# Seven-product first layer in a seventh chunk of a sorted-attention and expert-mixture kernel, with weight sums partly by adding transfers

## The chip, the core and the metric

The kernel runs on one core of a Trainium2 chip. The core has TensorE (PE, matrix multiply; its weight loads are listed apart as PEld), VectorE (DVE), ScalarE (ACT), GpSimd (POOL) and SyncE (SP); SP and POOL also issue transfers, which run on the core's 16 DMA engines. The time is the device time of the launch in microseconds, and the smaller the better.

## The reference

Block-sorted attention gives `x` (4 batches of 768 tokens, 512 wide), and four experts with weights per token give the output. What matters here is the second part:

```python
N, D, E, F = (3072, 512, 4, 1024)
p = domain_probs / (domain_probs.sum(-1, keepdims=True) + 1e-09)
out = np.zeros((N, D), dtype=np.float32)
for e in range(E):
    h = np.maximum(x @ w1[e], 0.0)
    out += p[:, e:e + 1] * (h @ w2[e])
```

The first layer is `x @ w1[e]`, the second layer `h @ w2[e]`.

## The kernel before

**Tiles and stages.** The 3072 tokens are worked off in 12 chunks of 256 tokens, three for each batch; chunk number `g` is batch `g // 3`, part `g % 3`. A chunk runs the first layer of all four experts into `Hb` (fp16, four blocks for each expert: two halves of the hidden width by two halves of the tokens), and then the second layer over all experts at once. The attention of later batches is woven into the chunks of batches 0 and 1, so that batches 2 and 3 have no attention left beside their chunks.

**Second layer.** A 2 x 2 block product in seven products instead of eight. Its sums of `w2` blocks are made once in place and in `T_e`; its sums of `Hb` blocks are made for each chunk by VectorE (`h_sums`, L734) into `Sb`, which has four areas `sm(0)` to `sm(3)`: `h_sums(e, 3)` writes `sm(2)`, `h_sums(e, 4)` writes `sm(3)`. The seven products are called b11, b21, n4, t1, t2, t3, b22 after the weight block that they use.

**First layer, two forms.** The plain form (`chunk_first`, L759) takes 32 matmuls of 256 columns for each expert, in two groups of 16; VectorE evicts a group by one instruction that applies ReLU and the token weight `pb` (L774). The seven-product form (`seven`, L1022) treats the layer as 2 x 2 blocks too: seven products p1 to p7, each 8 matmuls of 128 columns (L1032), linked by copies on ACT (L1052, L1059, L1067) and sums on VectorE (L1068, L1076). Two of the four result blocks are finished by VectorE (`finish`, L1038), two by ReLU on ACT and a multiplication on POOL (`finish2`, L1044 and L1045).

The seven-product form needs four sums of `w1` blocks for each expert (`input_sums`, L961): s1 = a21 + a22, s3 = a11 - a21, s2 = s1 - a11, s4 = a12 - s2. The first three lie in blocks of 1024 columns of `arena`, where the attention has its inputs, its mixing matrices and its output copy; s4 overwrites a21 in `w1`. It also needs four sums of token blocks for each chunk (`token_sums`, L975).

**Order.** Every engine runs its instructions in program order; the order was written by hand. In the chunks of batches 0 and 1, `chunk` (L783) calls `slot()` at fixed places: after each group of the first layer (slots 0 to 7) and after each product of the second layer (slots 8 to 14). `PLANS` names the attention steps for each (part, slot), and `PLAN_A` (L1175) the weight sums. With G0 = 6 (L972), chunks 3, 4 and 5 of batch 1 run in `chunk` with the plain form for all experts, and chunks 6 to 11 in `last_chunk` (L1088) with the seven-product form for all experts. `prepare_last` and `last_banks` close the attention's PSUM pool, then the chunks' pool, and open new ones for the seven-product form; each opening has one dummy matmul (L1000). `last_begin` (L1083) puts the first products of the next chunk's expert 0 ahead of the end of the present chunk.

**Buffers.** The temporaries of `seven` (u2, u3, t22, t12) lie in buffers that the attention no longer uses: a slot of the tag "xT", two of "vs" and one of "xsl". The normalised attention of the last two head pairs of batch 3 (`st_a`, L430) lies in `arena` blocks 4 and 5. The token weights `pb` have one buffer, loaded anew for each chunk by SP (L213).

Of the kernel before, what the change touches and what calls it, by code (L numbers as in the profile page):

```python
# [17 lines left out]
def kernel(  # L18
# [411 lines left out]
    def st_a(b, pr):  # L430
        if b == B - 1 and pr >= H // 2 - 2:
            xsl = arena[:, ds((pr + 2) * NB * 2 * D, NB * 2 * D)].rearrange("p (i h d) -> p i h d", i=NB, h=2)[0:BLK]
        else:
            xsl = att.tile([P, NB, 2, D], F16, name=f"xsl_{b}_{pr}", tag="xsl")[0:BLK]
        xsls[(b, pr)] = xsl
        vs = vss[(b, pr // 2)]
        for hh in range(2):
            ET = ETs[2 * (pr % 2) + hh]
            ps = psa([P, 2, 512], F32, f"ps_a_{b}_{pr}_{hh}")
            for i in range(NB):  # L440
                nc.tensor.matmul(  # L441
                    ps[:, i // HB, ds((i % HB) * VW, D + 1)],
                    ET[:, ds(i * BLK, P)],
                    vs[:, i, 2 * (pr % 2) + hh, 0:D + 1],
                    start=True, stop=True,
                )
            normalize(ps, xsl, hh)
# [286 lines left out]
    def h_sums(e, which):  # L734
        blk = lambda kh, tok: Hb[:, e, ds(kh * KH, KH), ds(tok * P, P)]
        sm = [Sb[:, n, e].rearrange("p (f x) -> p f x", f=KH) for n in range(4)]
        tt = nc.vector.tensor_tensor
        if which == 1:
            tt(sm[0], blk(0, 1), blk(1, 1), ALU.add)  # L739
        elif which == 2:  # L740
            tt(sm[1], sm[0], blk(0, 0), ALU.subtract)
        elif which == 3:
            tt(sm[2], blk(0, 0), blk(0, 1), ALU.subtract)
        else:
            tt(sm[3], blk(1, 0), sm[1], ALU.subtract)
# [37 lines left out]
    def chunk(b, c, slot, done=()):  # L783
# [13 lines left out]
        def product(n, lhs, rhs, pool=psm):  # L797
            ps = pool([P, DH], F32, f"ps_{n}_{b}_{c}")
            for e in es:
                if pool is last_bank and e == 2:  # L800
                    last["e0"][6]()
                for f in range(KH):
                    nc.tensor.matmul(  # L803
                        ps[:], lhs(e, f), Ts[e][rhs][:, f, :],
                        start=(e == es[0] and f == 0), stop=(e == E - 1 and f == KH - 1),
                    )
            return ps[:]
# [13 lines left out]
        if b or c:  # L821
            two = [psm([P, 2, 512], F32, f"ps_p{n}_{b}_{c}") for n in range(2)]
            bankA, bankB, bankC, bankQ = [two[n // 2][:, n % 2, 0:DH] for n in range(4)]
            if last:
                bankQ = last["Q"][1][:, 0:DH]
        if b:
            times(bankA, blk(0, 0), "b11", es)
            slot()
            times(bankB, blk(1, 0), "b21", es)
            slot()  # L830
            nc.scalar.copy(p1[:], bankA)
            tt(oa1, bankB, p1[:], ALU.add)
            times(bankQ, sm(0), "t1", es)
            nc.scalar.copy(p5[:], bankQ)
            slot()
            for e in es:
                h_sums(e, 3)
            times(bankA, sm(1), "t2", es, False)
            nc.scalar.copy(u2[:], bankA)
            slot()  # L840
            for e in es:
                h_sums(e, 4)
            times(bankC, blk(1, 1), "n4", es)
            nc.scalar.copy(ob1, bankC)
            slot()
            times(bankA, sm(2), "t3", es, False)
            tt(ob2, bankA, p5[:], ALU.add)
            tt(ob1, bankA, ob1, ALU.add)
            store(1, ob)
            slot()  # L850
            times(bankQ, sm(3), "b22", es, False, True, last["e0"][6] if last else None, 2 if last else None)
            tt(oa2, bankQ, u2[:], ALU.add)
            slot()
            store(0, oa)
            return
# [91 lines left out]
    def a_block(n):  # L947
        return arena[:, ds(n * AW, AW)].rearrange("p (k f) -> p k f", k=2)


    A_ORDER = (6, 7, 8, 0, 1, 2, 3, 4, 5, 9, 10, 11)
    As = []
    for e in range(E):
# [4 lines left out]
            "s1": a_block(A_ORDER[3 * e]), "s3": a_block(A_ORDER[3 * e + 1]), "s2": a_block(A_ORDER[3 * e + 2]),  # L958
        })

    def input_sums(e, n, half=None):  # L961
        a = As[e]
        dst, x, y, op = (
            ("s1", "a21", "a22", ALU.add), ("s3", "a11", "a21", ALU.subtract),
            ("s2", "s1", "a11", ALU.subtract), ("s4", "a12", "s2", ALU.subtract),
        )[n]
        part = slice(None) if half is None else slice(half, half + 1)
        nc.vector.tensor_tensor(a[dst][:, part], a[x][:, part], a[y][:, part], op)
# [3 lines left out]
    G0 = 2 * (R // 2)  # L972
    GN = B * (R // 2)

    def token_sums(g):  # L975
# [7 lines left out]
            "t1": t3[:, 0], "t2": t3[:, 1], "t3": t3[:, 2],  # L983
            "t4": wide[g % 2][:, 0:2 * P].rearrange("p (k x) -> p k x", k=2),
        }
        for dst, x, y in (("t1", "b12", "b11"), ("t2", "b22", "t1"), ("t3", "b22", "b12"), ("t4", "b21", "t2")):
            nc.vector.tensor_tensor(t[dst], t[x], t[y], ALU.subtract)
# [14 lines left out]
    def prepare_last():  # L1002

        last_banks(0)
        last["n"] = 1
        t = moe.tile([P, NKC, NB, BLK], F16, name="tmp7", tag="xT").rearrange("p k i x -> p (k i x)").bitcast(F32)
        room = [t[:, ds(n * 512, 512)] for n in range(3)]
        for m in range(2):
            t = att.tile([P, NB, 4, VW], F16, name=f"tmp7_{m}", tag="vs").rearrange("p i h w -> p (i h w)")
            t = t[:, 0:2048].bitcast(F32)  # L1010
            room += [t[:, 0:512], t[:, 512:1024]]
        t = att.tile([P, NB, 2, D], F16, name="tmp7_2", tag="xsl").rearrange("p i h d -> p (i h d)").bitcast(F32)
        room.append(t)
        for n, nm in enumerate(("u2", "u3", "t22", "t12")):
            last[nm] = room[2 * n:2 * n + 2]

    def last_bank(shape, dtype, name):
        n = last["n"]
        last["n"] += 1
        return last["Q"][2 - n % 2][:, 0:shape[1]]  # L1020

    def seven(g, e):  # L1022

        a, t, pb = As[e], Bs[g], pbs[divmod(g, R // 2)]
        X, Z, u2, u3, t22, t12 = [last[nm][e % 2] for nm in ("X", "Z", "u2", "u3", "t22", "t12")]
        X, Z, Q = X[:], Z[:], last["Q"][e][:]
# [30 lines left out]
        def p6():  # L1057
            product(X, "s2", "t2")
            nc.scalar.copy(u2, X)  # L1059
# [28 lines left out]
    def last_chunk(g):  # L1088
        b, c = divmod(g, R // 2)
        final = g == GN - 1  # L1090
        last["e0"][2]()
        if g == G0:
            last_banks(1)
        prs = [last["e0"]] + [seven(g, e) for e in range(1, E)]
        for e in range(1, E):
# [3 lines left out]
            if e > 1:  # L1099
                prs[e - 2][12]()  # L1100
# [6 lines left out]
            for n in late_sums.pop((g, e), ()):  # L1107
                input_sums(*n)
# [25 lines left out]
        nc.scalar.copy(p1[:], bankA)  # L1134
        now[3]()
# [7 lines left out]
        if final:  # L1143
            nc.sync.dma_start(o[:, 2 * c, 0:DH], oa1)
        h_sums(E - 1, 1)
# [3 lines left out]
        nc.scalar.copy(ob1, bankC)  # L1149
        for e in range(E):  # L1150
            h_sums(e, 4)
        product(bankQ, sm(0), "t1")
        nc.scalar.copy(p5[:], bankQ)
        product(bankA, sm(1), "t2", False)
        nc.scalar.copy(u2[:], bankA)
        for e in range(E):
            h_sums(e, 3)
        product(bankQ, sm(3), "b22", False, range(2))
        if not final:
            token_sums(g + 1)  # L1160
        product(bankA, sm(2), "t3", False)
        if not final:
            last_begin(g + 1)
# [3 lines left out]
        product(bankQ, sm(3), "b22", False, range(2, E), None if final else last["e0"][6], 3)  # L1167
# [8 lines left out]
        (1, 11, 0, 0), (1, 13, 0, 1), (2, 1, 0, 2), (2, 3, 1, 0), (2, 5, 1, 1), (2, 7, 1, 2),  # L1176
        (2, 8, 2, 0), (2, 9, 2, 1), (2, 10, 2, 2), (2, 10, 0, 3), (2, 11, 1, 3), (2, 11, 3, 0), (2, 12, 2, 3),
        (2, 13, 3, 1), (2, 14, 3, 2),
    ]
    late_sums = {(G0, 1): [(3, 3, 0)], (G0, 2): [(3, 3, 1)]}  # L1180
# [112 lines left out]
    for b in range(2):  # L1293
        for c in range(R // 2):
            done = (1, 2) if (b, c) == (0, 0) else ()
            at = [2 * len(done)]

            def slot(b=b, c=c, at=at):
                here = (c, at[0])
                for cc, n, f, *args in PLANS[b]:  # L1300
                    if (cc, n) == here:
                        f(*args)
                if b:
                    for cc, n, e, m in PLAN_A:
                        if (cc, n) == here:
                            input_sums(e, m)
                    if here == (R // 2 - 1, 7):
                        prepare_last()
                    if here == (R // 2 - 1, 12):
                        token_sums(G0)  # L1310
                    if here == (R // 2 - 1, 13):
                        last_begin(G0)
                at[0] += 1

            chunk(b, c, slot, done)
    for g in range(G0, GN):
# [29 lines left out]
```

The softmax here doesn't subtract the row's maximum and nothing guards it: scores larger than these inputs give would overflow.

## Time and profile before

| | us |
|---|---|
| median of 3 runs | 366.0 (365.18 to 366.91) |
| profiled execution, whole time | 364.59 |
| profiled execution, span from first to last instruction | 362.5 |

The granted clock of TensorE is 1.0 in the profiled execution. Some instants of its timeline, in us from the span's start:

| what | from | to |
|---|---|---|
| first matmul of chunk 5 (plain first layer) | 183.66 | |
| second layer of chunk 5, product b11 | 197.90 | |
| chunk 6, first product of expert 0, inside the end of chunk 5 | 208.38 | |
| second layer of chunk 6, product b11 | 222.13 | |
| same, chunk 7 | 246.86 | |
| last transfer issued by POOL (attention input) | 138.4 | 139.1 |
| POOL's first multiplication in `finish2` | 215.82 | |

How to read the profile: a row of a timeline has the start, the length, the engine, the line of the program, the operation, what it writes and reads with the shape, and how many instructions were merged; in brackets the idle time before it and what ended that. A row of windows has the window, its length, and then the busy time and the number of instructions of PE, PEld, DVE, ACT and POOL, the granted clock, the busy share of the DMA engines and GB/s. A row of transfers has the issuing queue, the number, the size of each and the median time from issue to landing. A row of waits has who waited for whom, the total, the number of times and the longest.

### The profile page before, as it was taken

What the parts mean: (1) busy time and instruction counts of PE and PEld (TensorE: products, weight loads), DVE (VectorE), ACT (ScalarE), POOL (GpSimd) and SP (SyncE); (2) the same over time, 40 slices, a digit from 0 to 9 for tenths busy, and PEclk for the clock granted to TensorE, in tenths of its full rate; (3) what the DMA queues carried; (4) which work ended last, traced back from release to release, by engine and by line L of the source; (5) the groups of instructions that cost most, each with busy time, mean ns of one, the idle gap of its engine ahead of it and who ended that gap; (6) DMA issues with size and microseconds to landing.
All of it is one profiled execution on the core that took longest, in us unless ns stands there. A gap on an engine that the chain in (4) does not pass through costs nothing.

```text
span 362.5 us, 10556 instructions
## 1 busy us (share of the span) xinstructions
PE 354.1 (98%) x4517; PEld 314.6 (87%) x4517; DVE 280.0 (77%) x559; ACT 157.7 (44%) x282; POOL 117.5 (32%) x134
## 2 busy tenths in 40 slices
PE   8799999999999999999999999999999999999996
PEld 8685857888888888988888899999999998999995
DVE  5753898779798676866799979868779679587794
ACT  2664430452424355367400157165283381561740
POOL 8882011655022420000000018137055082180470
PEclk9999999999999999999999999999999999999999
DMA  8999999999999999934450310310301101102101
GB/s 109 206 208 230 208 210 200 194 186 158 175 197 162 210 91 172 161 85 73 85 126 2 58 60 4 58 60 4 88 31 49 71 2 60 61 2 65 55 16 44
DMA packets 69753, 38.34 MB, mean 106 GB/s; under 512 B 40390, under 2 KB 64716, under 8 KB 69708
## 3 DMA queue, kind: packets, MB, share of 16 engines
q0 software_dynamic: 34640, 17.83, 38.5%
q1 hardware_dynamic: 35068, 19.85, 27.0%
q8 instruction: 35, 0.57, 0.6%
q14 instruction: 10, 0.08, 0.1%
HBM read 42.00 MB, written 6.34 MB: 133 GB/s over the span
## 4 chain that ended last, share of the span: by engine, by line
PE 86%; DVE 6%; DMA 5%; issue 1%; ACT 1%; POOL 1%; DVEq 0%; ACTq 0%
PE ps_Q L1121 20%; PE ps_h L768 18%; PE ps_p L753 13%; PE ps_X L1032 9%; PE ps_Z L1032 6%; PE ps_Q L1032 6%; DMA w<-in_moe_w_dram 4%; PE ps_o L696 3%; PE ps_p L803 2%; PE ps_h L661 1%; PE ps_s L406 1%; PE ps_a L441 1%; PE ps_k L387 1%; DVE Hb L774 1%; PE ps_v L354 1%
## 5 line engine op out<-in xcount | busy, mean ns | idle before, releaser
L1045 POOL TENSOR_TENSOR Hb<-tmp,pb 128x512 f16<-128x512 f32 x48 | 62.0, 1297 | 150.5 <-ACT tmp L1044 148.7
L768 PE MATMUL ps_h<-xT,w 128*128 128x256 f16 x672 | 78.4, 273 | 0.0
L768 PEld LDWEIGHTS <-w 128*128 128x128 f16 x672 | 64.5, 98 | 8.5
L774 DVE SCALAR_TENSOR_TENSOR Hb<-ps_h,pb 128x1024 f16<-128x1024 f32 x42 | 51.3, 1223 | 17.6 <-PE ps_h L768 17.4
L1032 PEld LDWEIGHTS <-w 128*128 128x128 f16 x768 | 46.6, 98 | 0.8
L1121 PEld LDWEIGHTS <-Sb 128*128 128x128 f16 x384 | 37.2, 98 | 4.1
L1032 PEld LDWEIGHTS <-arena 128*128 128x128 f16 x576 | 34.7, 98 | 0.1
L1044 ACT ACTIVATE tmp<-tmp 128x512 f32<-128x512 f32 x48 | 30.5, 635 | 6.4 <-DVE tmp L1076 5.2
L753 PEld LDWEIGHTS <-Sb 128*128 128x128 f16 x288 | 27.4, 98 | 4.2 <-issue 0.7
L1121 PEld LDWEIGHTS <-Hb 128*128 128x128 f16 x288 | 27.4, 98 | 2.9
L413 ACT ACTIVATE ET<-ps_s 96x768 f16<-96x768 f32 x24 | 18.1, 802 | 26.1 <-PE ps_s L406 25.8
L1032 PE MATMUL ps_X<-kT,arena 128*128 128x128 f16 x384 | 29.3, 219 | 0.0
L121 POOL DMA_DIRECT2D arena<-in_q_dram x24 | 19.9, 837 | 27.1 <-DMA qT<-arena 17.2
L396 ACT CAST kT<-ps_k 64x384 f16<-64x384 f32 x48 | 22.7, 473 | 13.2 <-PE ps_k L387 12.2
L739 DVE TENSOR_TENSOR Sb<-Hb 128x512 f16<-128x512 f16 x45 | 26.5, 609 | 0.0
L1068 DVE TENSOR_TENSOR tmp<-ps_Q,tmp 128x512 f32<-128x512 f32 x24 | 16.6, 691 | 12.2 <-ACT tmp L1067 8.0
L1121 PE MATMUL ps_Q<-w,Sb 128*128 128x256 f16 x192 | 24.7, 273 | 0.0
L1121 PE MATMUL ps_Q<-w,Hb 128*128 128x256 f16 x192 | 23.9, 273 | 0.0
L1052 ACT COPY ps_X<-ps_Z 128x512 f32<-128x512 f32 x24 | 13.7, 570 | 22.8 <-PE ps_Z L1032 22.4
L753 PEld LDWEIGHTS <-Hb 128*128 128x128 f16 x216 | 20.6, 98 | 3.1 <-issue 0.3
L1121 PE MATMUL ps_Q<-T,Sb 128*128 128x256 f16 x192 | 22.9, 273 | 0.0
L1059 ACT COPY tmp<-ps_X 128x512 f32<-128x512 f32 x24 | 14.1, 586 | 12.2 <-PE ps_X L1032 12.2
(189 smaller groups left out, 605.3 us busy)
## 6 DMA issues: line engine op xcount, KB each, us to landing
w<-in_moe_w_dram POOLq DMA_DIRECT2D x7, 1024.0 KB, 27.0
pb<-p_dram SPq DMA_DIRECT2D x12, 512.0 KB, 5.5
arena<-in_k_dram POOLq DMA_DIRECT2D x8, 384.0 KB, 8.6
arena<-in_v_dram POOLq DMA_DIRECT2D x8, 384.0 KB, 9.6
vs<-arena SPq DMA_DIRECT2D x36, 66.0 KB, 5.2
arena<-in_q_dram POOLq DMA_DIRECT2D x24, 96.0 KB, 6.7
out_dram<-ob SPq DMA_DIRECT2D x9, 256.0 KB, 2.0
out_dram<-oa SPq DMA_DIRECT2D x8, 256.0 KB, 2.4
```

What stands on the lines that cost most here:

```text
L121: nc.gpsimd.dma_start(t[:, h // 2, :, h % 2, :], q[b, h].rearrange("(t p) d -> p t d", p=P))
L396: nc.scalar.copy(kT[ds(D * hh, D), r], pk[ds(D * r, D), hh].rearrange("p a (i c) -> p a i c", c=CP),)
L413: nc.scalar.activation(ETs[2 * (pr % 2) + hh][:, 0:S].rearrange("c (a x) -> c a x", a=2), pss[hh][0:BLK, :, 0:HS], AF.Exp, bias=0.0, scale ...
L739: tt(sm[0], blk(0, 1), blk(1, 1), ALU.add)
L753: nc.tensor.matmul(ps, lhs(e, f), Ts[e][rhs][:, f, :], start=(first and e == es[0] and f == 0), stop=(done and e == es[-1] and f == KH - 1 ...
L768: nc.tensor.matmul(ps[:, f, :], w1sb[e][:, kc, ds((4 * g + f) * P, P)], xT[:, kc, ds(2 * c * P, 2 * P)], start=(kc == 0), stop=(kc == NKC ...
L774: nc.vector.scalar_tensor_tensor(out=Hb[:, e, ds(4 * g, 4), :], in0=ps[:], scalar=0.0, op0=ALU.max, in1=pb[:, ds(e, 1), :].broadcast_to([P ...
L1032: nc.tensor.matmul(dst[:, ds(f * P, P)], a[lhs][:, k, ds(f * P, P)], t[rhs][:, k, :], start=(first and f == 0 and k == 0), stop=(f == KH - ...
L1044: nc.scalar.activation(src, src, AF.Relu, bias=0.0, scale=1.0)
L1045: nc.gpsimd.tensor_tensor(Hb[:, e, ds(i * KH, KH), ds(j * P, P)], src.rearrange("p (f x) -> p f x", f=KH), pb[:, ds(e, 1), ds(j * P, P)].b ...
L1068: tt(t22, Q, u3, ALU.add)
L1121: nc.tensor.matmul(ps, lhs(e, f), Ts[e][rhs][:, f, :], start=(first and e == 0 and f == 0), stop=(e == E - 1 and f == KH - 1), skip_group_ ...
```

## The change

Chunk 5 (`G0 = 2 * (R // 2) - 1`) moves from `chunk` to `last_chunk`. Its expert 0 keeps the plain form; experts 1, 2 and 3 take the seven-product form. With it come these edits:

- The sum s2 is replaced by its negative n2 = s3 - a22, and the token sum t2 by its negative, so that n2 x n2 is the same product; s4 = a12 + n2.
- `input_sums` has two forms. With `vector=True`, VectorE makes the sum as before. Otherwise ScalarE writes a copy (or the negative) of one operand to the destination, and a transfer issued by POOL adds the other operand to it (`accum_op`). Experts 1 to 3 have twelve sums at slots of chunks 4 and 5: expert 1's s1, s3 and n2 are made by VectorE, the other nine by ScalarE and a transfer. Expert 0's four sums are made by ScalarE and a transfer at hooks in the second layer of chunk 5.
- Expert 0's s1 and s3 take two blocks in the area of `sm(2)`, its n2 `arena` block 3. `xsl` of the last two head pairs moves from `arena` to the area of `sm(3)`. For that, `h_sums` 3 and 4 write in place in `Hb` in all chunks of batches 1 to 3, and the products t3 and b22 read `Hb` there.
- The token sums of chunk 5 stand at the last slot of chunk 4. The two changes of PSUM pools stand after the plain expert and after the first four products of expert 1. The temporaries of chunk 5 take two slots of "vs" and two of "xsl".

```diff
-    def h_sums(e, which):
+    def h_sums(e, which, own=False):
...
-            tt(sm[2], blk(0, 0), blk(0, 1), ALU.subtract)
+            tt(blk(0, 1) if own else sm[2], blk(0, 0), blk(0, 1), ALU.subtract)
...
-            tt(sm[3], blk(1, 0), sm[1], ALU.subtract)
+            tt(blk(1, 0) if own else sm[3], blk(1, 0), sm[1], ALU.subtract)
...
-    A_ORDER = (6, 7, 8, 0, 1, 2, 3, 4, 5, 9, 10, 11)
+    def a_block(n):
+        home, at = (arena, n) if n < 12 else (Sflat, n - 8)
+        return home[:, ds(at * AW, AW)].rearrange("p (k f) -> p k f", k=2)
+    A_ORDER = (12, 13, 3, 6, 7, 8, 0, 1, 2, 9, 10, 11)
...
-    def input_sums(e, n, half=None):
+    def input_sums(e, n, vector=False):
         a = As[e]
+        dst, x, sign, y = (
+            ("s1", "a21", 1.0, "a22"), ("s3", "a21", -1.0, "a11"), ("n2", "a22", -1.0, "s3"), ("s4", "a12", 1.0, "n2"),
         )[n]
+        if vector:
+            nc.vector.tensor_tensor(a[dst], a[y], a[x], ALU.add if sign > 0 else ALU.subtract)
+        else:
+            nc.scalar.mul(a[dst], a[x], sign)
+            nc.gpsimd.dma_start(a[dst], a[y], accum_op=ALU.add)
...
-    G0 = 2 * (R // 2)
+    G0 = 2 * (R // 2) - 1
...
+    HOOKS = {"p1": [(0, 0)], "p2": [(0, 1)], "c": [(0, 2)], "q": [(0, 3)]}
+    def hook(g, at):
+        if g == G0:
+            for e, n in HOOKS[at]:
+                input_sums(e, n)
...
-    def last_chunk(g):
+    def last_chunk(g, slot=None):
...
+        lead = int(g == G0)
+        if lead:
+            chunk_first(b, c, [0], 0, slot)
+            last_banks(0)
+            last_tmp(g)
+            prs = {1: seven(g, 1)}
+            for n in (1, 5, 2, 6):
+                prs[1][n]()
             last_banks(1)
+        else:
+            last["e0"][2]()
+            prs = {0: last["e0"]}
+        for e in range(1 + lead, E):
+            prs[e] = seven(g, e)
...
         nc.scalar.copy(p1[:], bankA)
+        hook(g, "p1")
...
         tt(oa1, bankB, p1[:], ALU.add)
...
+        hook(g, "p2")
...
         nc.scalar.copy(ob1, bankC)
+        hook(g, "c")
...
         nc.scalar.copy(p5[:], bankQ)
+        hook(g, "q")
...
     PLAN_A = [
-        (1, 11, 0, 0), (1, 13, 0, 1), (2, 1, 0, 2), (2, 3, 1, 0), (2, 5, 1, 1), (2, 7, 1, 2),
-        (2, 8, 2, 0), (2, 9, 2, 1), (2, 10, 2, 2), (2, 10, 0, 3), (2, 11, 1, 3), (2, 11, 3, 0), (2, 12, 2, 3),
-        (2, 13, 3, 1), (2, 14, 3, 2),
+        (1, 9, 1, 0, True), (1, 9, 1, 1, True), (1, 11, 1, 2, True),
+        (1, 8, 2, 0), (1, 9, 2, 1), (1, 11, 3, 0), (1, 12, 2, 2), (1, 13, 3, 1), (1, 14, 3, 2),
+        (2, 0, 1, 3), (2, 0, 2, 3), (2, 1, 3, 3),
     ]
-    late_sums = {(G0, 1): [(3, 3, 0)], (G0, 2): [(3, 3, 1)]}
...
+                if here == (1, 14):
+                    token_sums(G0)
```

An entry of `PLAN_A` is part, slot, expert and sum (0 s1, 1 s3, 2 n2, 3 s4).

## The prediction

> **What bounds the kernel now.** I read the engine totals first, then the chain of work that ended last, then TensorE in order of time around the edit, then who is idle there, and last the transfers.
>
> ```profile
> PE 354.1 (98%) x4517; PEld 314.6 (87%) x4517; DVE 280.0 (77%) x559; ACT 157.7 (44%) x282; POOL 117.5 (32%) x134
> ...
> PE 86%; DVE 6%; DMA 5%; issue 1%; ACT 1%; POOL 1%; DVEq 0%; ACTq 0%
> ```
>
> TensorE carries 86% of the chain. The windows between chosen instants show whether it ever pauses where the edit is:
>
> ```profile
> 183.66:197.69 14.03, 14.03 (x135) 12.52 (x132) 13.49 (x21) 0.00 (x0) 0.00 (x0) 1.00 0.29 60
> 197.90:208.38 10.48, 10.48 (x97) 9.39 (x96) 10.44 (x23) 1.49 (x4) 0.00 (x0) 1.00 0.29 50
> 211.47:222.13 10.66, 10.66 (x187) 10.45 (x185) 9.87 (x16) 7.60 (x14) 4.99 (x4) 1.00 0.08 28
> 236.20:260.93 24.73, 24.73 (x340) 23.46 (x337) 19.43 (x40) 12.76 (x24) 10.32 (x8) 1.00 0.18 45
> ```
>
> Columns: window, length, busy PE, PEld, DVE, ACT, POOL. Busy PE equals the length in every row: from 183.66 us on, TensorE does not wait. So the edit can gain only matmul time, and loses whatever wait it makes. ACT and POOL are idle in chunk 5 (second index 2 of batch 1), POOL since the last load; the first two rows show it, and so do the waits:
>
> ```profile
> POOL Hb L1045 <- ACT tmp L1044: 77.7, 4, 76.7
> ACT p L831 <- PE ps_p L753: 22.0, 2, 21.1
> ```
>
> The price of both kinds of first layer stands in TensorE's timeline:
>
> ```profile
> 131.45 1.91 PE L768 MATMUL ps_h<-xT,w 128*128 128x256 f16 x16
> 133.20 0.49 PE L354 MATMUL ps_v<-arena 128*128 128x384 f16 x2
> ...
> 239.27 0.61 PE L1032 MATMUL ps_X<-ET,w 128*128 128x128 f16 x8
> 239.72 0.61 PE L1032 MATMUL ps_Q<-xT,w 128*128 128x128 f16 x8
> ```
>
> From start to start: 16 plain matmuls in 1.75 us (109.2 ns each), 8 small ones in 0.447 us (55.9 ns each; mean over many such rows). The widths in the row overlap and are not used.
>
> **What the Trainium skill says.** "DMA: Bandwidth & Descriptors", section "Anatomy of one DMA — SWDGE (gpsimd) path", fits a transfer from GpSimd with 2.0 us plus bytes over 436e3. For the 256 KB of one adding transfer (128 x 1024 f16) that is 2.6 us. The trace doesn't agree for the transfers POOL issues: none lands that fast.
>
> ```profile
> arena<-in_v_dram POOLq DMA_DIRECT2D x8, 384.0 KB, 9.6
> vs<-arena SPq DMA_DIRECT2D x36, 66.0 KB, 5.2
> arena<-in_q_dram POOLq DMA_DIRECT2D x24, 96.0 KB, 6.7
> out_dram<-ob SPq DMA_DIRECT2D x9, 256.0 KB, 2.0
> ```
>
> These are medians; the fastest POOL load of 96 KB landed after 4.4 us, the fastest of 384 KB after 5.6 us. Both come from HBM, change the type, and share busy queues. The same page, "Two DMAs through the same engine are not ordered", says that the issuing engine must wait on a transfer's semaphore before it issues one that reads the result. No POOL transfer here reads another's result, so the trace is silent; but POOL does wait in its queue (it sat 4.6 us on TensorE before the load at 134.0). Prices: "ScalarE: Activation LUTs", section "What ACT_TABLE_LOAD costs", gives 186 ns + 0.833 ns per element, so 1.04 us for 1024 elements (an estimate). The rows agree: 768 elements took 802 ns, predicted 826; a 96x1024 copy took 1008 ns.
>
> **The change part by part.**
> *First layer.* Per expert, plain is 32 x 109.2 = 3.494 us, seven-product is 56 x 55.9 = 3.128 us. Three experts: 3 x 0.366 = **1.10 us less** on TensorE. Chunk 5 starts at 183.66 in both. Before, its second layer starts at 197.90, one dummy matmul (0.21 us) ahead of it; after, both dummies and 19 of the 21 small products are ahead, so it starts at 183.66 + 3.494 + 0.42 + 19 x 0.447 = 196.07, and the last two products (0.89) lie inside it.
>
> *Three weight sums by VectorE (expert 1).* 3 x 0.60 us (pace of the L968 rows) at slots 9 and 11 of chunk 4. Two go between the normalise that ends at 173.73 and `oa1`; h_sums(3) then ends near 176.6 and is needed at 178.92. Hidden. The sum at slot 11 takes the place of one at 178.27. The sum at 183.28 goes away (0.60).
>
> *Nine weight sums as ScalarE scale plus adding transfer.* On ACT 9 x 0.95 (they overlap by 0.09). At slots 8 and 9 they follow the cast that ends at 170.86; p1's copy moves from 171.81 to 172.75, needed when bankA is reused at 174.39. At 11 the scale runs 176.7 to 177.7, ahead of the copy at 178.58. The rest follow the two exps that end at 180.58 and end at 186.4; the first new ACT copy is due at 187.95. All hidden; without the idle ACT they would cost 8.6 us.
>
> *Token sums earlier.* Four at 0.23 = 0.93 us (208.09 to 209.02 shows them) now follow the last normalise. VectorE: output sum 183.28, normalise to 185.29, sums to 186.22, the two ReLU evictions of expert 0 to 187.4 and 188.55. TensorE needs the second at the second bank change, 187.15 + 0.21 + 4 x 0.447 = 189.15. Margin 0.6 us; each further microsecond of VectorE lag costs the rest.
>
> *In-place sums, the other arena blocks, the moved bank changes.* Same instructions and widths. h_sums(4) writes a block whose product b21 ended long before, h_sums(3) one that no earlier product reads: nothing new to wait for. The temporaries have three pairs for three experts, so none is reused in the chunk. I take 0 (bounds -0.2 to +0.3).
>
> *The adding transfers.* Each takes POOL about 0.8 us to issue (740 to 848 ns in the load rows). Let L be the time from POOL's start to landing. POOL runs in order; a transfer that needs another's landing holds all behind it. The order at the boundary, with ACT's times: e2's s1 at 171.9, s3 at 172.9, e3's s1 at 177.8, e2's n2 at 181.65, e3's s3 at 182.6. Then e3's n2 must wait for s3: issued 182.7 + L. Behind it e1's s4 is issued at 183.5 + L and lands at **183.5 + 2L**; e2's s4 at 184.3 + 2L; e3's s4, which waits for n2, at 182.8 + 3L. TensorE wants them at 192.03, 195.16 and 198.24 (each product 0.447, counted from 187.15). So the first stalls at L over 4.27, by 2L - 8.53. The finish multiplications on POOL queue behind; the first is ready near 192.3, so they wait only if L passes 4.3.
>
> The second chain is expert 0's four sums, spread over the second layer. I shift the rows of chunk 6 (b11 at 222.13) by -26.08, so that b11 falls on 196.05. s1: ACT 198.8 to 199.9, lands 199.95 + L, wanted 208.74. Its issue delays POOL's last finish by 0.3 us, still before VectorE's sum at 202.4. s3: POOL at 202.05, after that finish. n2 waits for s3, is issued at 202.15 + L, lands at **202.15 + 2L**; its product p6 stands before the last quarter of b22, at 209.63. It stalls at L over 3.74, by 2L - 7.48. s4 lands at 202.25 + 3L, wanted at 213.64 plus that stall.
>
> *The size of L.* Below: POOL's load at 134.0 had its first packet 1.2 us later (packet records of the trace); the 1024-byte packets of the SP queue take 46 ns, 16 per engine are 0.74 us; with the end about 2.3. Above: 4.4 to 5.6, the fastest POOL loads. An adding transfer reads two operands and there is no HBM, so I take **L = 3.3** alone (twice the packet time), and 4.2 for s3 of expert 0, whose packets meet the load of the next weights `pb` (issued near 202, landing after 5.4). Then n2 of expert 0 lands near 209.9: stall **0.3 us**.
>
> *Sum.* -1.10 + 0.3 = **-0.8 us**. The profiled execution took 364.59 us (span 362.5); it becomes 363.8. Their median is 366.0, so I predict 365.2.
>
> **Rivals.**
> 1. *All transfers hidden* (L below 3.7 with all traffic): -1.10, 364.9. For it: queue share is 0.08 to 0.3 there, and a plain 256 KB store lands in 2.0. Against: `pb` in the way.
> 2. *Slower: the dependent transfers decide.* Place: POOL's queue, s3 to n2 to s4. At L = 4.2 the stalls eat the gain. At L = 5: 1.5 us at s4 of e1, 2.5 at n2 of e0, 1.1 at s4 of e0, minus 1.10 = +4.0, 370.0. It passes 0.5% from L = 4.55. For it: every POOL transfer in this trace took 4.4 or more. Against: those came from HBM with type change, one after another.
> 3. *VectorE late at the bank change*: a lag of 1 us beyond my count stalls TensorE by 0.4, -0.7 with nothing else, 365.3. For it: VectorE is 96% busy in the first window. Against: that load was the weight sums and evictions that go.
> 4. *The small products are not faster* (weight loads bound them): 0, 366.0. The windows speak against it: 24.73 us is 224 x 55.9 + 112 x 109.2 = 24.75.
>
> **How the numbers follow.** Forecast (small stall) 0.40, rival 1 0.22, rival 2 0.30 (about a fifth of it under 0.5%), rival 3 0.06, rival 4 0.02. About 0.5% (1.8 us) is what a measurement of this kernel can tell from no change. The whole possible gain is 0.3%, so faster than that takes luck of the runs, whose spread is 365.18 to 366.91: 0.07 of the first two cases. Slower 0.28 with a little scatter, same 0.65. The likeliest case has its own range 364.3 to 366.2; out to rival 2 at L = 5 the range is 364.0 to 370.0.
>
> **What would show it.** In the profile after: 168 small and 32 plain matmuls between 183.7 and 196; b11 at 196.07. A wait of TensorE before p3 of expert 1 (near 192) or p6 of expert 0 (near 209.6), released by a DMA, is rival 2; its length gives L. The landing row of the adding transfers gives L at once: over 4.5 makes the prediction wrong. A wait at the second dummy matmul released by VectorE is rival 3. From chunk 6 on, 24.73 us per chunk must stand.

## The result, and the profile after

The changed kernel takes 377.37 us (median of 4 runs, 377.14 to 380.41), the kernel before 365.59 us beside it (364.62 to 366.91). The ratio is 1.0339, 95% interval 1.0276 to 1.0402: slower by 11.8 us, where 365.2 was forecast and 370.0 was the end of the range. The profiled execution after took 377.29 us; its span is 375.4 us, 12.9 more than before.

The page of the kernel after, engine totals, granted clock of TensorE in 40 slices, and the chain that ended last:

```profile
PE 357.0 (95%) x4589; PEld 317.4 (85%) x4589; DVE 275.8 (73%) x555; ACT 178.5 (48%) x310; POOL 139.7 (37%) x153
...
PEclk9999999999999999999998989999999999999999
...
PE 71%; DMA 19%; DVE 7%; ACT 1%; issue 1%; POOL 0%; DVEq 0%; SPq 0%; POOLq 0%
```

TensorE fell from 86% to 71% of the chain, and transfers rose from 5% to 19%. TensorE is busy 2.9 us *longer* although it has fewer matmul columns to run, and two slices show a lower clock. The windows of the kernel after, over the same pieces of work as before (columns as there; "DMA share" is the last but one):

```profile
186.01:204.51 18.50, 14.53 (x193) 13.52 (x189) 10.16 (x20) 8.79 (x14) 7.37 (x7) 0.91 0.83 132
204.51:223.10 18.59, 14.96 (x155) 12.91 (x153) 12.57 (x27) 8.34 (x15) 8.73 (x8) 1.00 0.39 86
223.10:235.05 11.95, 11.95 (x187) 11.91 (x185) 7.98 (x13) 8.09 (x15) 5.85 (x5) 0.86 0.22 47
249.12:273.85 24.73, 24.73 (x339) 23.46 (x337) 19.43 (x40) 12.75 (x24) 10.34 (x8) 1.00 0.13 44
```

The first row is chunk 5 up to b11, the second from b11 to p2 of the next chunk's expert 0, the third the rest of chunk 6's first layer. Busy PE no longer equals the length in the first two, and in the first and third the clock is below 1. The last row, a later chunk, has 24.73 us as before: nothing is lost behind chunk 6's first layer. The waits name the places (kernel after; two waits near the start, which the kernel before has too, are left out):

```profile
PE ps_Q L1037 <- DMA w<-arena: 3.7, 1, 3.7
PE ps_X L1037 <- DMA arena<-Sb: 3.6, 1, 3.6
PE ps_s L406 <- DMA qT<-arena: 1.6, 1, 1.6
...
PE ps_p L753 <- DVE oa L828: 0.9, 1, 0.9
```

The first is p3 of expert 1 waiting for expert 1's s4, the second p6 of expert 0 (chunk 6) waiting for expert 0's n2, the last t2 of chunk 4 waiting for VectorE's output sum. The third lies before 74 us, where the two programs are the same. TensorE's timeline after the first wait:

```profile
198.85 0.70 PE L1037 MATMUL ps_Q<-xT,w 128*128 128x128 f16 x8 [3.69 <-DMA w<-arena]
199.35 1.06 PE L1037 MATMUL ps_Z<-xT,w 128*128 128x128 f16 x8
200.20 1.06 PE L1037 MATMUL ps_X<-kT,arena 128*128 128x128 f16 x8
201.05 1.06 PE L1037 MATMUL ps_Q<-kT,arena 128*128 128x128 f16 x8
201.91 0.98 PE L1037 MATMUL ps_Z<-xT,w 128*128 128x128 f16 x8
202.72 0.61 PE L1037 MATMUL ps_X<-kT,arena 128*128 128x128 f16 x8
```

From start to start a product takes 0.85 us here instead of 0.447, that is 107 ns per matmul instead of 55.9, until 202.72. The granted clock in the window of this stretch is 0.56.

From starts of the same work in both traces the 12.9 us come apart so:

| stretch | before | after | more |
|---|---|---|---|
| up to the scores matmul (L406) near 73 us | 72.67 | 73.99 | +1.32 |
| from there to the first matmul of chunk 5 | 110.99 | 112.02 | +1.03 |
| chunk 5 to p2 of expert 0 of chunk 6 | 27.81 | 37.09 | +9.28 |
| from there to b11 of chunk 6 | 10.66 | 11.95 | +1.29 |
| rest | 140.37 | 140.35 | -0.02 |

Of the second row, 0.95 is the wait of t2.

The third and fourth row, +10.57 together, hold: the matmuls saved (-1.10), the two late products (+3.85 and +3.74, start to start against 0.447), the slow stretches behind them (five products in 3.87 and 3.86 us instead of 2.24, +1.6 each), 0.37 at p2 of expert 1 (which waits for ScalarE's copy of p1) and 0.23 one product after the bank change, and 0.38 inside t1, whose weight loads wait for VectorE's block sums. That is 10.7.

Why the two products were late is on POOL (timeline of the kernel after; a row of L968 begins when POOL starts to issue an adding transfer):

```profile
184.15 0.90 POOL L968 DMA_DIRECT2D arena<-arena  x1 [2.67 <-ACT arena L967]
185.10 1.19 POOL L968 DMA_DIRECT2D arena<-w  x1
192.74 0.90 POOL L968 DMA_DIRECT2D arena<-arena  x1 [6.44 <-ACT tmp L1064]
193.32 2.75 POOL L968 DMA_DIRECT2D w<-arena  x2
...
210.80 1.67 POOL L968 DMA_DIRECT2D Sb<-w  x1
218.85 0.89 POOL L968 DMA_DIRECT2D arena<-Sb  x1 [6.38 <-ACT ps_X L1057]
222.72 1.19 POOL L968 DMA_DIRECT2D w<-arena  x1 [2.98 <-DMA arena<-Sb]
```

Expert 3's s3 is issued at 185.10 and lands 7.1 us later; only then its n2 can go (192.74), and expert 1's s4, which needs neither, stands behind it in POOL's queue until 193.32 and lands 5.5 us later, at 198.8, when p3 starts. Expert 0's s3 (210.80) lands 7.5 us later, n2 (218.85) another 3.3: at 222.2 p6 starts. In the brackets ScalarE is named as the releaser of 192.74 and 218.85, with copies that the two transfers don't use. Their own ScalarE steps (L967) had ended by 185.75 and 212.17; the last thing they waited for was the landing of s3, at 192.2 and 218.3. In the first case a semaphore wait of POOL's queue that began at 185.4 lasted 6.82 us, up to that landing. The times from issue to landing (medians, kernel after):

```profile
arena<-w POOLq DMA_DIRECT2D x4, 256.0 KB, 5.9
w<-arena POOLq DMA_DIRECT2D x4, 256.0 KB, 5.3
...
arena<-arena POOLq DMA_DIRECT2D x2, 256.0 KB, 4.2
...
Sb<-w POOLq DMA_DIRECT2D x2, 256.0 KB, 5.7
...
arena<-Sb POOLq DMA_DIRECT2D x1, 256.0 KB, 3.3
```

All thirteen together: 3.3 at least, 4.9 in the median, 7.5 at most.

### The profile page after: what moved, and what is told of

Its sections match the earlier page's. It is cut to its first block, busy times and chain, and to the rows that moved or that the text cites. A ratio compares the mean times of both kernels' runs of the same rounds, so it can differ in the third digit from the quotient of the medians.

```text
span 375.4 us, 10784 instructions
## 1 busy us (share of the span) xinstructions
PE 357.0 (95%) x4589; PEld 317.4 (85%) x4589; DVE 275.8 (73%) x555; ACT 178.5 (48%) x310; POOL 139.7 (37%) x153
## 4 chain that ended last, share of the span: by engine, by line
PE 71%; DMA 19%; DVE 7%; ACT 1%; issue 1%; POOL 0%; DVEq 0%; SPq 0%; POOLq 0%
PE ps_Q L1141 22%; PE ps_h L768 12%; PE ps_p L753 10%; PE ps_X L1037 10%; PE ps_Z L1037 7%; DMA arena<-in_q_dram 7%; DMA w<-in_moe_w_dram 6%; PE ps_Q L1037 6%; DMA qT<-arena 2%; DMA w<-arena 1%; PE ps_s L406 1%; DVE Sb L739 1%; DVE Hb L774 1%; PE ps_k L387 1%; PE ps_a L441 1%
## 5 line engine op out<-in xcount | busy, mean ns | idle before, releaser
L1050 POOL TENSOR_TENSOR Hb<-tmp,pb 128x512 f16<-128x512 f32 x40 | 51.3, 1290 | 77.7 <-ACT tmp L1049 76.4
L768 PE MATMUL ps_h<-xT,w 128*128 128x256 f16 x576 | 67.8, 273 | 0.0
L1141 PEld LDWEIGHTS <-Hb 128*128 128x128 f16 x560 | 53.4, 98 | 5.6
L774 DVE SCALAR_TENSOR_TENSOR Hb<-ps_h,pb 128x1024 f16<-128x1024 f32 x36 | 44.0, 1223 | 18.9 <-PE ps_h L768 18.7
L1141 PE MATMUL ps_Q<-w,Hb 128*128 128x256 f16 x336 | 43.4, 273 | 0.0
L1141 PE MATMUL ps_Q<-T,Hb 128*128 128x256 f16 x224 | 26.7, 273 | 0.0
L1049 ACT ACTIVATE tmp<-tmp 128x512 f32<-128x512 f32 x40 | 25.4, 634 | 1.2 <-DVE tmp L1073 1.0
L753 PEld LDWEIGHTS <-Hb 128*128 128x128 f16 x232 | 21.9, 98 | 3.3 <-issue 0.3
L1141 PEld LDWEIGHTS <-Sb 128*128 128x128 f16 x224 | 21.8, 98 | 3.1 <-DVE Sb L739 0.6
L1050 POOL TENSOR_TENSOR Hb<-tmp7x,pb 128x512 f16<-128x512 f32 x14 | 19.2, 1373 | 5.0 <-ACT tmp7x L1049 5.0
L1043 DVE SCALAR_TENSOR_TENSOR Hb<-ps_X,pb 128x512 f16<-128x512 f32 x27 | 18.5, 685 | 3.1 <-PE ps_X L1037 3.1
```

What stands on the lines that cost most here:

```text
L753: nc.tensor.matmul(ps, lhs(e, f), Ts[e][rhs][:, f, :], start=(first and e == es[0] and f == 0), stop=(done and e == es[-1] and f == KH - 1 ...
L768: nc.tensor.matmul(ps[:, f, :], w1sb[e][:, kc, ds((4 * g + f) * P, P)], xT[:, kc, ds(2 * c * P, 2 * P)], start=(kc == 0), stop=(kc == NKC ...
L774: nc.vector.scalar_tensor_tensor(out=Hb[:, e, ds(4 * g, 4), :], in0=ps[:], scalar=0.0, op0=ALU.max, in1=pb[:, ds(e, 1), :].broadcast_to([P ...
L1043: nc.vector.scalar_tensor_tensor(out=Hb[:, e, ds(i * KH, KH), ds(j * P, P)], in0=src.rearrange("p (f x) -> p f x", f=KH), scalar=0.0, op0= ...
L1049: nc.scalar.activation(src, src, AF.Relu, bias=0.0, scale=1.0)
L1050: nc.gpsimd.tensor_tensor(Hb[:, e, ds(i * KH, KH), ds(j * P, P)], src.rearrange("p (f x) -> p f x", f=KH), pb[:, ds(e, 1), ds(j * P, P)].b ...
```

## The experiments

The theory after the result was that dependent adding transfers, slower than estimated, hold TensorE twice, and that the slow stretches follow from the holding. The rivals: VectorE, the in-place sums, or the new order on TensorE cost the time, and the waits for transfers only cover it.

The profiled executions differ by up to 2.0 us in when they reach the scores matmul near 73 us, before anything that the change touches. So traces are compared below by the rest of the span, from there to the end: 289.8 us in the kernel before, 301.4 in the kernel after.

### All sixteen sums on VectorE

```diff
-    def input_sums(e, n, vector=False):
+    def input_sums(e, n, vector=True):
```

> All sixteen weight sums by VectorE at the same places; no scale on ScalarE, no adding transfer. If the chain of dependent adding transfers makes the loss (two waits of 3.7 and 3.6 us, and about 1.6 and 1.5 us of matmuls at half speed after them), both waits and both slow stretches go: 377.3 - 10.4 = 367, less or more by what thirteen more sums of 0.6 us do to VectorE. If the loss comes from the new order itself (bank changes, token sums, in-place sums, temporaries), it stays near 377.

Measured: 368.63 us (368.17 to 369.83), ratio 1.0112 (1.0085 to 1.014); span 366.4, rest of the span 294.0, clock 1.000. The waits of TensorE in this kernel, from 150 us on those of 0.4 and more:

```profile
PE ps_p L753 <- DVE oa L828: 1.5, 1, 1.5
PE ps_X L1003 <- DVE Hb L774: 1.3, 1, 1.3
...
PE ps_Q L1141 <- DVE Hb L743: 0.9, 1, 0.9
...
PE ps_a L441 <- DVE Sb L423: 0.4, 1, 0.4
```

Without adding transfers, and the ScalarE steps that feed them, both long waits and both slow stretches are gone. They had cost 10.8 us (the two late products and the two slow stretches above); the rest of the span falls by 7.4, since VectorE's waits now take more. These too cost more than the matmuls save: t2's output sum, the second bank change (the place of rival 3), t3's block sums, and the attention's normalise ahead of chunk 5 (L423).

### The in-place sums alone

The kernel before, with `h_sums` 3 and 4 written in place in batches 1 to 3:

```diff
-            tt(sm[2], blk(0, 0), blk(0, 1), ALU.subtract)
+            tt(blk(0, 1) if own else sm[2], blk(0, 0), blk(0, 1), ALU.subtract)
...
-        product(bankA, sm(2), "t3", False)
+        product(bankA, blk(0, 1), "t3", False)
```

> The kernel before with the one edit that h_sums 3 and 4 write in Hb in place in batches 1 to 3. If in-place sums cost nothing, as the prediction had it: 365.6, ratio 1.00. If they make new waits (the weight loads of t3 and b22 behind VectorE), each of nine chunks pays, and some of the microsecond that is lost in chunk 4 after the change shows here.

Measured: 364.83 us, ratio 0.9993 (0.9978 to 1.0009). The in-place sums cost nothing that shows.

### TensorE kept busy while it waits

The kernel after, with 66 and 64 matmuls of 128 columns into unused banks ahead of the two late products:

```diff
             prev[4]()
+            if lead and e == 2:
+                fill(last["Q"][1], 66)
             prev[3]()
...
+        def p6_next():
+            if lead:
+                fill(last["Q"][2], 64)
+            last["e0"][6]()
```

> The changed kernel with 66 and 64 dummy matmuls of 128 columns (3.7 and 3.6 us) on a free PSUM bank ahead of the two products that wait. The waits stay as long in time, but TensorE isn't idle in them. If the matmuls at 106 ns instead of 56 after each wait come from TensorE's idleness, they go: 377.3 - 3.1 = 374.2. If they come from something else that is busy then (transfers, weight reads), the time stays at 377.3.

Measured: 374.53 us (373.27 to 376.23), ratio 1.0285 (1.0246 to 1.0323); span 371.5, rest of the span 299.5, that is 1.9 less than after. TensorE's timeline:

```profile
193.02 3.85 PE L1090 MATMUL ps_Q<-w 128*128 128x128 f16 x66
196.87 0.62 PE L1037 MATMUL ps_Q<-xT,w 128*128 128x128 f16 x8
197.33 0.61 PE L1037 MATMUL ps_Z<-xT,w 128*128 128x128 f16 x8
197.78 0.61 PE L1037 MATMUL ps_X<-kT,arena 128*128 128x128 f16 x8
```

The product starts as late as in the kernel after (124.85 us behind the scores matmul, there 124.86), but those behind it run at 0.45 us each. The transfers beside them are as busy as there (DMA share 0.48 against 0.52), so it is idleness that slows them, not contention. "TensorE: Matmul & The Clock Gate" of the Trainium skill states this in "Part 1: The HAM clock gate (the "warmup" mystery)": after an idle window of about 3.4 us the array runs at half clock, until it has been busy for about as long, 106.7 ns for 128 columns. The traces agree: 107 ns, for 3.9 us. All runs side by side show where it begins: waits of 3.16 to 3.87 us were followed by a slow stretch, waits of 2.04 and 2.35 were not. The shortest of these is a little under the page's 3.4 us; the measurement decides. Part of the gain went back: s4 of expert 0 made a third wait, 1.34 us, that ended at 223.95, since TensorE now arrives there earlier; 3.2 less 1.3 is the 1.9 above. That the time still came near the expected one is in part luck: this kernel's profiled execution was 2.0 us ahead near 73 us, for no reason that the change gives.

### Without the load of the next token weights

Chunk 6 uses chunk 5's `pb` here; the 512 KB load is left out.

```diff
-            pbs[divmod(g + 1, R // 2)] = load_p(*divmod(g + 1, R // 2))
+            pbs[divmod(g + 1, R // 2)] = pbs[(b, c)] if lead else load_p(*divmod(g + 1, R // 2))
```

> The changed kernel in which chunk 6 uses the token weights of chunk 5 (the load of 512 KB behind chunk 5 is left out, so chunk 6's output is another). If that load is what makes the transfer of expert 0's s3 land after 7.5 us instead of 3.9, n2 is issued about 3.6 us earlier, the second wait (3.6 us) shrinks to below 0.5 and its slow stretch goes: about 372.3. If the landing time is POOL's own, the wait stays and so does 377.3.

Measured: 374.91 us (two runs, 373.18 and 376.63), ratio 1.0279 (1.0215 to 1.0343); span 371.4, rest of the span 299.2, that is 2.2 less than after. Expert 0's s3 landed after 4.3 us instead of 7.5 (7.2 and 7.6 in the two other kernels that keep expert 0's transfers and the load), and the wait before p6 fell from 3.58 to 0.31. "DMA: Bandwidth & Descriptors", "Issuing engines are not separate DMA queues", says that transfers of all engines interleave on the same 16 DMA engines; the trace agrees: with the load beside it, this transfer took 3.2 us longer. VectorE was busy in all of the 4.3 us here, as over the same stretch in the kernel after, so it isn't what stretched the transfer. But the expected time was missed, as the third link of the chain came up (TensorE's timeline):

```profile
217.27 0.62 PE L1037 MATMUL ps_X<-kT,arena 128*128 128x128 f16 x8 [0.31 <-DMA arena<-Sb]
...
223.81 0.62 PE L1037 MATMUL ps_Q<-xT,w 128*128 128x128 f16 x8 [2.35 <-DMA w<-arena]
```

s4, issued at 217.79 after n2, took 6.0 us. I had counted the wait that goes and not the one behind it.

### The order of the transfers alone

Expert 1's s4 issued ahead of expert 3's s3, and expert 1's two vector sums one slot later:

```diff
-        (1, 9, 1, 0, True), (1, 9, 1, 1, True), (1, 11, 1, 2, True),
-        (1, 8, 2, 0), (1, 9, 2, 1), (1, 11, 3, 0), (1, 12, 2, 2), (1, 13, 3, 1), (1, 14, 3, 2),
-        (2, 0, 1, 3), (2, 0, 2, 3), (2, 1, 3, 3),
+        (1, 10, 1, 0, True), (1, 10, 1, 1, True), (1, 11, 1, 2, True),
+        (1, 8, 2, 0), (1, 9, 2, 1), (1, 11, 3, 0), (1, 12, 1, 3), (1, 12, 2, 2), (1, 13, 3, 1), (1, 14, 3, 2),
+        (2, 0, 2, 3), (2, 1, 3, 3),
```

> The changed kernel with two edits of order only: expert 1's s4 is issued ahead of expert 3's s3 (so it isn't held in POOL's queue by the wait of n2 on s3), and expert 1's two vector sums stand one slot later, behind the output sum oa. Theory of the queue: the wait of 3.7 us before p3 of expert 1 goes, and what is late next is expert 2's s4 or expert 3's n2, still behind that wait, 1 to 2.5 us; the 1.0 us before t2 goes; the second wait near 220 stays: 377.3 - 1.0 - 2 - (1.6 if the rest is short) = 373 to 375. If the landing time alone makes the wait and not the queue, p3 of expert 1 still waits over 3 us.

Measured: 373.18 us (372.79 to 374.23), ratio 1.0223 (1.0197 to 1.0249); span 371.6, rest of the span 298.7, that is 2.7 less than after. TensorE's waits in this kernel, the longest of the changed part:

```profile
PE ps_X L1037 <- DMA arena<-Sb: 3.2, 1, 3.2
PE ps_X L1037 <- DMA arena<-arena: 2.0, 1, 2.0
PE ps_Q L1141 <- DVE Sb L739: 1.4, 1, 1.4
```

The wait of t2 for the output sum is gone, and so is the one of expert 1's p3; so both had the cause given. Late next are expert 3's n2 (2.0), expert 2's s4 (0.6) and, further on, VectorE's block sums for t1 (1.4). Expert 3's s3, now behind two more transfers, landed after 9.5 us instead of 7.1. Order alone moves the stall to the next dependent transfer.

### No transfer that depends on another near its use

The transfers that remain are those of chunk 4, with expert 0's s1 at its end, and expert 0's s3 at the start of chunk 5, all issued by 187.3; the sums that depend on late ones (s4 of experts 2 and 3, n2 and s4 of expert 0) go to VectorE at places where it has time.

```diff
-    HOOKS = {"p1": [(0, 0)], "p2": [(0, 1)], "c": [(0, 2)], "q": [(0, 3)]}
+    HOOKS = {"p1": [], "p2": [], "c": [], "q": []}
...
+            for n in LATE.get(e, ()) if lead else ():
+                input_sums(*n, True)
...
+        (1, 8, 1, 0, True), (1, 8, 1, 1, True), (1, 10, 1, 2, True),
+        (1, 8, 2, 0), (1, 9, 2, 1), (1, 10, 3, 0), (1, 11, 3, 1), (1, 12, 1, 3), (1, 12, 2, 2), (1, 13, 3, 2),
+        (1, 14, 0, 0), (2, 0, 0, 1),
...
+    LATE = {2: [(2, 3)], 3: [(3, 3)]}
```

Further, three of the token sums move to slot 12 of chunk 4, and p1 and p5 of expert 1 stand between the two plain groups of expert 0.

> The change with its first layer kept and its sums laid elsewhere: the late dependent ones (e2's s4, e3's s4, e0's n2 and s4, e1's first three) by VectorE in its gaps, the rest by adding transfers issued 10 us or more ahead of their use; three of the four token sums earlier; p1 and p5 of expert 1 between the two plain groups of expert 0. If the matmul saving is real and the loss lay only in waits, no wait of TensorE over 0.5 us is left from 150 us on and the kernel gains up to 1.1 us: ratio 0.997 to 1.000. If the first layer as such costs (bank changes, temporaries), it stays over 1.003.

Measured: 364.23 us against 364.79 (22 and 27 runs), ratio 0.9991 (0.9976 to 1.0007): the loss is gone, and no gain is measured. The rest of the span is 289.6 us. From the first matmul of chunk 5 to b11 of chunk 6 it takes 38.16 us (27.89 up to p2), where the kernel before takes 38.47 (27.81, with one dummy matmul, 0.21, beyond that point). TensorE's waits from 150 to 240 us, all that are listed:

```profile
PE ps_X L1003 <- DVE Hb L774: 0.4, 1, 0.4
PE ps_Q L1037 <- DVE tmp L1073: 0.2, 1, 0.2
```

The first is at the second bank change, 0.42 us, the other 0.18.

### One product moved

In the last kernel p5 of expert 1 goes behind the second plain group, so that the bank change comes one product later:

```diff
-                    for n in (1, 5):
+                    for n in (1,):
                         prs[1][n]()
...
-            for n in (2, 6):
+            for n in (5, 2, 6):
```

> The kernel of e6_repaired with one product moved: only p1 of expert 1 stands between the two plain groups of expert 0, p5 follows with p2 and p6. The second bank change then comes 0.447 us later behind the last plain group, so its wait of 0.42 us for VectorE's eviction (L774) should go to about 0. Theory (the rest of the gain was held back by that wait and one of 0.18): chunk 5 takes 27.5 instead of 27.9 us from its first matmul to p2 of the next chunk, the span is near 361.8, the time near 363.8, ratio about 0.998. Rival (VectorE itself is the bound of chunk 5 there, so that the wait only moves): the same 0.4 us turns up at a later wait for VectorE and the span stays at 362.2.

Measured: 363.67 us against 364.54 (12 and 17 runs), ratio 0.9972 (0.9959 to 0.9984). The windows of this kernel, up to b11, up to p2, and from there to 222.40, which is 0.50 us behind the start of chunk 6's b11 (221.90):

```profile
184.08:197.08 13.00, 12.81 (x193) 11.85 (x189) 10.20 (x17) 7.81 (x13) 6.32 (x7) 1.00 1.17 168
197.08:211.62 14.54, 14.54 (x155) 13.19 (x153) 13.71 (x31) 4.61 (x10) 4.93 (x4) 1.00 0.15 46
211.62:222.40 10.78, 10.78 (x191) 10.73 (x189) 8.29 (x14) 8.34 (x16) 5.51 (x5) 1.00 0.11 40
```

Chunk 5 takes 13.00 + 14.54 = 27.54 us, as expected, and busy PE equals the length but for 0.19. The wait at the bank change is gone, but for 0.13 us from start to start. From the first matmul of chunk 5 to b11 of chunk 6 this kernel takes 37.82 us, 0.65 less than the kernel before; the rest of the span, 289.2, is 0.6 less. This version is 0.3% faster than the kernel before, with an interval that leaves 1 out. The step from the last kernel to this one is shown by the traces (0.34 us); the intervals of the two overlap. Its adding transfers were no faster (4.7, 7.1 and 10.2 us at least, in the median and at most); nothing waits for them.

## Why the prediction was wrong, by its steps

In short: the forecast let every adding transfer land after 3.3 to 4.2 us. The two s3 landed after 7.1 and 7.5, and what stood behind each had to wait for that and then for a landing of its own. So TensorE stood still twice, and a cost that the prediction didn't have, matmuls at half speed after each stand, came on top.

**"The size of L" failed.** The forecast took 3.3 us, and 4.2 for expert 0's s3. Measured: 3.3 for the quickest of thirteen, 4.9 in the median, and 7.1 and 7.5 for the two s3 on which everything hung. The sign that the prediction had named for its being wrong, over 4.5, came; the estimate of 2.6 us, which it had set aside, lay under all thirteen. The figure of 3.3 was that of a transfer alone, and there it was near: expert 0's n2 took 3.3, and its s3 without the load of `pb` 4.3. What was mis-sized for expert 0's s3 is the traffic: the only correction for it was 0.9 us, on this one transfer, and the load of `pb` alone made 3.2. The upper bound, 4.4 to 5.6, was set by the fastest loads of POOL, which bound the quickest case and not the typical one; the medians in the same rows were 6.7 and 9.6. What stretched expert 3's s3 to 7.1 stays open. While it was under way the DMA engines were nearly always busy, and SP's queue, with transposes and an output store, took more of their time (64%) than POOL's (47%). That speaks for traffic here too, but no run took these away.

**"The adding transfers" was right in its mechanism, places and formulas.** It named expert 1's s4 behind expert 3's n2, and expert 0's n2. Its issue times held: expert 3's s3 was forecast for 182.6, chunk 5 began 2.35 us late, and s3 was issued at 185.10. With the measured landings, 7.1 + 5.5 in place of 2L, the first stall is 12.6 - 8.53 = 4.1 (measured 3.85); with 7.5 + 3.3 the second is 10.8 - 7.48 = 3.3 (measured 3.74). Those two are 7.6 us where the sum had 0.3. This is rival 2, given 0.30; its own time, 370.0 at L = 5, was too low for the L that came and for the next item.

**A term was missing: matmuls behind a long wait run at half speed.** No step priced it; it made 3.2 us for the two stalls. Keeping TensorE busy took it away.

**"Three weight sums by VectorE" was wrong in its deadline.** It checked `h_sums(3)` for t3, and p1's copy for bankA, and found both in time. t2 also waits for the output sum `oa` (L828), which stands behind expert 1's two sums at slot 9: 0.95 us. Moving them one slot took it away.

**"Nine weight sums as ScalarE scale"**: no wait of TensorE for the scales was seen; but p2 of expert 1 waited for ScalarE's copy of p1, 0.37 us start to start, with only one product, p5, between the two. The prediction checked only when the first copy would be due. Its reading that ScalarE is idle in chunk 5 holds for the first of the two rows alone: the second has four copies, 1.49 us.

**"Token sums earlier" and rival 3**: no wait at the second bank change in the kernel after, as forecast. With more on VectorE it appeared, 1.3 us in the first experiment and 0.4 in the sixth, where 0.6 us of margin had been counted for the kernel after.

**"First layer" and "In-place sums" held.** With the seven-product form and no stall, chunk 5 took 27.54 us up to p2; 27.81 + 0.21 - 1.10 would be 26.92, and the pauses that the last kernel's timeline still shows from start to start (0.35, 0.13, 0.09 and 0.08) are the difference. The kernel before has pauses too in that stretch up to chunk 6's b11, so that 0.65 of the 1.10 us were gained in all. The in-place sums cost nothing that shows. Rival 4 is out: from b11 of chunk 6 on, the rest takes 140.35 us against 140.37, and the small products 0.447 us.

Of the 12.9 us, 1.3 lie before 74 us, in work that the change leaves alone. The six variants of the changed kernel reach that instant at 72.0 to 73.1, with at most 0.2 us of the wait for qT that took 1.6 there; what made that wait wasn't tried and stays open. So 11.6 of the 12.9 us are put down to the change, and 1.3 are not explained.

## What to carry to other kernels

A chain of transfers in which each waits for the landing of the last is as late as the sum of its landings, and holds everything behind it in the issuing queue; so the transfers that depend on nothing go first and early, and a step near its use goes to an engine with a known time. The landing time of a transfer kind that the profile doesn't show should be bounded by the typical and the slow ones of its kin under the same traffic, not by the fastest. And a wait of TensorE can cost more than its length: the four of 3.16 to 3.87 us without filling were followed by 1.3 to 1.6 us more of slow matmuls, the two of 2.04 and 2.35 by none. Other lengths weren't measured here.

## What the runs showed of the hardware that was not expected

- An adding transfer of 256 KB within the core's memory lands after 3.3 to 7.5 us in the kernel after, and after up to 10.2 us in the last kernel, where seven are issued between 177.6 and 187.7 and nothing waits. Those that write into `w1` (the four s4) took 4.8 to 6.1 us in the kernel after; no run shows why.
- In the kernel after POOL takes 0.9 us to issue one whose two sides are both blocks outside `w1` (`arena`, `Sb`), and 1.2 to 2.0 us where one side is in `w1`; the forecast had 0.8 for all.
- Half speed of TensorE after waits of 3.16 to 3.87 us, for 3 to 4 us; with matmuls in the wait it doesn't come.
